# A spectral filter and a low-rank mixer on one core: which engine issues batch 1's spectrum stores, and in which slot its loads back stand

## The chip, the core and the metric

The kernel runs on one core of a Trainium2 chip. The core has five instruction streams that run side by side and meet only at semaphores: TensorE (PE), which multiplies matrices into PSUM banks; VectorE (DVE), ScalarE (ACT) and GpSimd (POOL), which compute elementwise; and SyncE (SP), which here does nothing but issue DMA transfers. ACT and POOL can issue DMA transfers too. Each stream is executed in order: an instruction that waits holds everything behind it on the same stream, and a DMA issue is such an instruction.

The metric is the device time of one execution in microseconds (us), as the median of several runs.

## What is computed

`x` has 8 batches of 3136 positions and 256 channels. The reference filters each channel in the frequency domain along the 3136 positions, and then applies a low-rank mixer along the positions and an MLP along the channels:

```python
X = np.fft.rfft(x, axis=1)
Y = X * (filt_r + 1j * filt_i)[None, :, :]
y = np.fft.irfft(Y, n=3136, axis=1)
u = y + (y.transpose(0, 2, 1) @ U @ V).transpose(0, 2, 1)      # rank 32
out = u + np.maximum(u @ w_ch1, 0.0) @ w_ch2                   # 256 -> 1024 -> 256
```

## The kernel before

**The transform.** 3136 is 64 x 49. A transform along the positions is done as a 64-point stage, a 49-point stage with the twiddle factors in its matrices, the filter, and the two stages back. For batches 1 to 7 the steps are these:

1. `f1_units`: PE multiplies a batch's `xt` tiles by the 64-point matrix (`pf`), ACT or DVE copies the result to `asb`, and a DMA stores it in the DRAM tensor `c1`. The stores of batch 1 are issued by SP, those of the later batches by POOL.
2. `load_a` (lines 466 to 470): SP loads a quarter of it back in another order, as one of three `a2` tiles (98 partitions x 8 frequencies x 256 channels), in two transfers, one of 96 partitions and one of 2. A quarter, number `gi` of 4, is 8 of the 32 frequency classes `NS`.
3. `stream` (lines 515 to 546): for each of 16 steps `m`, so 4 steps to a quarter, PE does the 49-point stage (`px`, line 488), DVE multiplies by the filter (`uv`), from batch 2 on POOL adds two halves (`y`), and PE does the 49-point stage back (`pi`, line 524). `pi` runs `LAG` = 2 steps behind `px`. ACT copies `pi` to one of two `esb` tiles (line 528), and behind the fourth copy of a quarter `esb` is stored in the DRAM tensor `c2`, again as one transfer of 96 partitions and one of 2 (line 531). This is the spectrum store.
4. `load_e` (lines 472 to 481): SP loads the quarter back in another order into the tiles `e2`, in three transfers (two at line 476, one at line 481). It can start only when both parts of the spectrum store have landed.
5. `h1_unit` (lines 552 to 589): when all four quarters of `e2` are there, PE projects them on the rank of the mixer (`ph`, line 566, 49 matmuls), ACT scales that (`h1`), PE folds it (`pn`), ACT copies it (`hz`), and DVE and four SP transfers spread it over further partitions of `e2` (lines 577 to 588).

Batch 0 does all this within the core's memory (`first_f1`, `first_mid`) before the main loop.

**The main loop** (lines 849 to 868) goes through the batches in groups of 4 row blocks. For each group, `make_u` forms `ut` with the last transform stage and the mixer (`u_part`, line 609), `mm1` does the first half of the MLP into 8 tiles `h` (line 683, ReLU on ACT at line 691), and `mm2` the second half of the group before (line 709 or 754). The result goes through DVE to `och` and by DMA to `out`.

**The order.** Instructions are recorded as the program writes them, and each engine executes its own in this order; no scheduler moves them. What belongs to the transform of later batches is woven into the main loop by hand, through numbered slots: `put(slot, ...)` files a piece of work and `run(slot)` records it. A group has 8 slots, a batch 48 (`SB`), and slots 0 to 47 lie under batch 0's MLP. For the work around the change the slots are these: the last copy of batch 1's quarters and with it the spectrum store at slots 14, 19, 25 and 30 (`steps`, line 809, and `put(t, mid)`); batch 2's `load_a` at slots 19, 29, 39 and 48 (line 832); `h1_unit` of batch 1 from slot 39 on (line 817); and batch 1's `load_e` where lines 821 to 828 put it, with `b` = 0 in that place (it counts the batches of the stream from 0):

```python
if k >= LAG and m % GP == GP - 1:
    t += 6 if b > 1 else 4 if b else 2
    late = SB * b + 13
    if b and t < late:
        ...
    else:
        put(t, one(load_e, b + 1, m // GP))
```

So `load_e` of batch 1 stands in slots 16, 21, 27 and 32, two behind its store.

SP's stream in this stretch is, in order: `load_a` of batch 1's first three quarters; store 0; `load_a` of batch 1's fourth quarter; e 0; store 1; `load_a` of batch 2's quarter 0; e 1; store 2; e 2; `load_a` of batch 2's quarter 1; store 3; e 3; `load_a` of batch 2's quarter 2. A store waits for ACT's copies, an e for the landing of its store, and `load_a` of batch 2's quarter 0 for the landing of batch 2's `c1` stores. Every transfer that SP or ACT issues signals its landing on one of eight completion semaphores, which the program gives out in turn, and it is not issued before the transfer that had this semaphore last has landed.

Of the kernel before, what the change touches and what calls it, by code (L numbers as in the profile page):

```python
# [16 lines left out]
DM = 256  # L17
# [72 lines left out]
def kernel(  # L90
# [11 lines left out]
    nc = tc.nc  # L102
# [11 lines left out]
    c2 = [nc.dram_tensor(f"c2_{b}", (64, RD), F16, kind="Internal") for b in range(nb)]  # L114
# [7 lines left out]
    def bank(tag, name):  # L122
        return ps.tile([128, 512], F32, tag=tag, bufs=BUFS[tag], name=name)
# [14 lines left out]
    def natural(ap):  # L138

        return ap.rearrange("p (r i h a) -> p r h i a", i=4, h=2, a=32)  # L140

    def split(ap):

        return ap.rearrange("p (r h i a) -> p r h i a", i=4, h=2, a=32)
# [318 lines left out]
    def spec(t, gi, p, n):  # L463
        return bass.AP(tensor=t, offset=gi * KG * 2 * RD + p * DM, ap=[[DM, n], [2 * RD, KG], [1, DM]])
# [18 lines left out]
    def forward(m, a2, xtags):  # L483
        ml = m % (KG // 2)
        px = bank(xtags[m % len(xtags)], "px")
        for sl in range(2):
            s = 2 * m + sl
            nc.tensor.matmul(px[:, sl * DM:(sl + 1) * DM], t2[:, s * 128:(s + 1) * 128],  # L488
                             a2[:, (2 * ml + sl) * DM:(2 * ml + sl + 1) * DM],
                             start=True, stop=True, skip_group_check=True)  # L490
        return px
# [23 lines left out]
    def stream():  # L515
        pend = []

        def i1(b, m, y, esb):
            pi = bank("f", "pi")
            nf = 2 if b == 1 else 1  # L520
            for sl in range(2):
                for fi in range(nf):
                    g, o = (4 * m + 2 * sl + fi) * 98, fi * 512 + sl * DM
                    nc.tensor.matmul(pi[0:98, sl * DM:(sl + 1) * DM], g12[:, g:g + 98],  # L524
                                     y[:, o:o + DM], start=(fi == 0), stop=(fi == nf - 1),
                                     skip_group_check=True)
            gi, ml = divmod(m, KG // 2)
            nc.scalar.copy(split(esb[:, ml * 512:(ml + 1) * 512]), natural(pi[0:98, :]))  # L528
            if ml == KG // 2 - 1:
                for p, n in ((0, 96), (96, 2)):  # L530
                    nc.sync.dma_start(spec(c2[b], gi, p, n),
                                      esb[p:p + n].rearrange("p (k d) -> p k d", d=DM))

        for b in range(1, nb):
            for m in range(NS // 2):
                gi, ml = divmod(m, KG // 2)
                if ml == 0:
                    esb = sb.tile([98, KG * DM], F16, tag="esb", bufs=2, name="esb")
                y = (both_products if b == 1 else product)(m, forward(m, st[b]["a"][gi], ("x",)))
                if len(pend) == LAG:  # L540
                    i1(*pend.pop(0))
                pend.append((b, m, y, esb))
                yield
        for p in pend:
            i1(*p)
            yield

    def one(load, *a):
        load(*a)
        yield  # L550
# [227 lines left out]
    def put(slot, gen):  # L778
        sched.setdefault(int(slot + 0.5), []).append(gen)
# [6 lines left out]
    NP = NS // 2  # L786
# [31 lines left out]
    for k, t in enumerate(steps):  # L818
        put(t, mid)
        b, m = divmod(k - LAG, NP)  # L820
        if k >= LAG and m % GP == GP - 1:
            t += 6 if b > 1 else 4 if b else 2
            late = SB * b + 13
            if b and t < late:
                put(max(t, SB * b - 1), one(load_e, b + 1, m // GP, (0,)))
                put(late, one(load_e, b + 1, m // GP, (1,)))
            else:
                put(t, one(load_e, b + 1, m // GP))
    for b in range(1, nb):
        for gi in range(NS // KG):  # L830
            t = steps[NP * (b - 1) + GP * gi]
# [67 lines left out]
```

## Time and profile before

| what | value |
|---|---|
| median of 3 runs | 538.48 us (536.94 to 539.28) |
| the profiled execution | 540.42 us |
| its span, first to last instruction | 537.5 us |
| granted TensorE clock, mean over the span | 0.983 |
| DMA moved, share of the 16 engines busy | 94.58 MB; 38.4% by POOL's queue, 37.8% by SP's |

How to read the profile. The first lines of its page give the span and each engine's busy time. PEld is the weight load of TensorE, which overlaps its matmuls. The chain of waits follows the work that ended last back through whatever released each step; a piece "DMA c<-esb" is the time from the issue of that transfer to its landing. The timeline lists an engine's instructions in order of time: start, duration, engine, line, operation, output and input by the program's tile names without their numbers (so `c` is `c1` or `c2`, `e` is `e2`, `a` is `a2`), shapes and count; a bracket at the end gives the idle time in front of it and what ended it. SPq stands for the stream of SP, whose instructions are DMA issues: their duration is that of the issue, not of the transfer. The view by windows gives for each stretch of time its length, the busy time and number of instructions of PE, PEld, DVE, ACT and POOL in this order, the granted TensorE clock (1.00 is full speed), the mean busy share of the 16 DMA engines and the GB/s that they moved. All times in these views count from the first instruction.

### The profile page before, as it was taken

The numbers are of one execution on the slowest core, as the hardware profiler recorded it, in microseconds if no ns is written. First come the engines' busy times: TensorE is split into PE (matmuls) and PEld (weight loads), VectorE is DVE, ScalarE is ACT, GpSimd is POOL, SyncE is SP. The second block draws the span as 40 slices with busy tenths as digits, with TensorE's granted clock in tenths as the row PEclk, the third lists the DMA queues.
The fourth block names the chain that finished last, engine by engine and source line by source line (L and its number), as shares of the span: only waits on it lengthen the run. The fifth ranks groups of instructions, "written<-read, shape, count | busy, mean of one in ns | idle before, by whom it ended". The sixth has DMA issues, their size and how long they took to land.

```text
span 537.5 us, 11370 instructions
## 1 busy us (share of the span) xinstructions
PE 501.6 (93%) x4022; PEld 305.5 (57%) x4022; DVE 396.5 (74%) x567; ACT 380.0 (71%) x777; POOL 287.9 (54%) x406
## 2 busy tenths in 40 slices
PE   3865899988999999999999999999999999999995
PEld 3754467755776776555555555555554555454444
DVE  6885377773787766888898878887999887335663
ACT  2666866764877867888888778888787777765541
POOL 7776553434466444676668567684756565313000
PEclk9889999997999999999999999999999999999999
DMA  8999999856988758896979798896876584643324
GB/s 132 189 198 209 181 203 222 215 158 178 203 210 208 196 121 236 189 243 142 249 196 235 185 187 215 207 229 161 201 184 153 126 193 115 141 105 80 75 67 104
DMA packets 118426, 94.58 MB, mean 176 GB/s; under 512 B 52961, under 2 KB 100770, under 8 KB 118370
## 3 DMA queue, kind: packets, MB, share of 16 engines
q0 software_dynamic: 21936, 42.52, 38.4%
q1 hardware_dynamic: 96434, 51.35, 37.8%
q8 instruction: 31, 0.51, 0.4%
q14 instruction: 25, 0.20, 0.1%
HBM read 56.85 MB, written 48.17 MB: 195 GB/s over the span
## 4 chain that ended last, share of the span: by engine, by line
PE 74%; DMA 10%; DVE 6%; ACT 3%; POOL 3%; issue 2%; SPq 1%; DVEq 0%; POOLq 0%; ACTq 0%
PE phh L683 26%; PE po L754 20%; PE po L709 7%; PE px L488 5%; PE pi L524 4%; PE pu L609 4%; DMA c<-esb 3%; DVE uv L509 3%; PE pf L449 3%; DMA xt<-in_x_dram 2%; PE ph L566 2%; DMA a<-c 2%; DMA g<-gd 1%; DMA c<-asb 1%; DVE uv L507 1%
## 5 line engine op out<-in xcount | busy, mean ns | idle before, releaser
L691 ACT ACTIVATE h<-phh 128x512 f16<-128x512 f32 (+1 forms) x391 | 205.6, 578 | 71.9 <-PE phh L683 68.9
L683 PE MATMUL phh<-ut,w 128*128 128x512 f16 x768 | 198.3, 380 | 0.9 <-ACT ut L676 0.5
L512 POOL TENSOR_TENSOR y<-uv 128x512 f16<-128x512 f16 x96 | 111.2, 1159 | 118.7 <-DVE uv L509 84.9
L754 PE MATMUL po<-h,w 128*128 128x512 f16 x560 | 143.8, 379 | 0.0
L509 DVE TENSOR_TENSOR uv<-px,ft 64x512 f16<-64x512 f32 x192 | 132.1, 688 | 2.6
L683 PEld LDWEIGHTS <-w 128*128 128x128 f16 x832 | 78.6, 98 | 78.1 <-issue 3.5
L507 DVE TENSOR_TENSOR uv<-px,ft 128x512 f16<-128x512 f32 x96 | 65.3, 680 | 48.7 <-PE px L488 42.9
L772 POOL DMA_DIRECT2D out_dram<-och x120 | 70.5, 594 | 40.7 <-DVE och L764 36.9
L528 ACT CAST esb<-pi 98x512 f16<-98x512 f32 x112 | 65.9, 589 | 36.3 <-PE pi L524 33.6
L754 PEld LDWEIGHTS <-w 128*128 128x128 f16 x560 | 51.6, 98 | 53.2 <-issue 1.1
L763 DVE TENSOR_TENSOR tt<-po,ut 128x512 f32<-128x512 f32 x70 | 48.4, 692 | 32.5 <-PE po L754 30.8
L709 PE MATMUL po<-w,h 128*128 128x256 f16 x448 | 58.7, 274 | 0.0
L488 PE MATMUL px<-a,t 98*128 98x256 f16 x256 | 50.0, 277 | 7.7 <-DVE uv L509 3.6
L455 ACT CAST asb<-pf 128x512 f16<-128x512 f32 (+1 forms) x83 | 48.1, 580 | 9.2 <-PE pf L449 8.2
L764 DVE STREAM_TRANSPOSE och<-tt 128x512 f32<-128x512 f32 x70 | 49.8, 711 | 2.4
L709 PEld LDWEIGHTS <-h 128*128 128x128 f16 x448 | 42.9, 99 | 10.8 <-issue 1.4
L496 DVE TENSOR_TENSOR uv<-px,ft 128x1024 f16<-128x1024 f32 x32 | 38.4, 1222 | 12.2 <-PE px L488 11.8
L488 PEld LDWEIGHTS <-t 98*128 98x128 f16 x256 | 22.9, 100 | 35.0 <-DVE uv L509 11.8
L449 PE MATMUL pf<-xt,w 128*128 128x512 f16 (+1 forms) x91 | 34.8, 384 | 5.6 <-DMA xt<-in_x_dram 4.4
L673 ACT CAST ut<-pu 128x512 f16<-128x512 f32 x70 | 38.1, 609 | 0.0
L524 PE MATMUL pi<-y,g 128*98 128x256 f16 x192 | 36.9, 273 | 0.7 <-POOL y L512 0.7
L153 POOL DMA_DIRECT2D xt<-in_x_dram x50 | 30.3, 613 | 4.2 <-DMA xt<-in_x_dram 1.6
(92 smaller groups left out, 440.9 us busy)
## 6 DMA issues: line engine op xcount, KB each, us to landing
xt<-in_x_dram POOLq DMA_DIRECT2D x46, 256.0 KB, 6.5
a<-c SPq DMA_DIRECT2D x28, 384.0 KB
c<-esb SPq DMA_DIRECT2D x28, 384.0 KB
e<-c SPq DMA_DIRECT2D x56, 192.0 KB
out_dram<-och SPq DMA_DIRECT2D x160, 64.0 KB
c<-asb POOLq DMA_DIRECT2D x30, 256.0 KB, 4.8
out_dram<-och POOLq DMA_DIRECT2D x120, 64.0 KB, 3.3
out_dram<-och POOLq DMA_DIRECT2D x24, 256.0 KB, 4.5
```

The costliest lines, as they stand in the source:

```text
L449: nc.tensor.matmul(pf[:, 0:w], w64[:, :], xt[:, n0 * DM:n0 * DM + w], start=True, stop=True)
L488: nc.tensor.matmul(px[:, sl * DM:(sl + 1) * DM], t2[:, s * 128:(s + 1) * 128], a2[:, (2 * ml + sl) * DM:(2 * ml + sl + 1) * DM], start=Tru ...
L507: nc.vector.tensor_mul(uv[:, 0:512], px[:, :], ft[:, a:a + 512])
L509: nc.vector.tensor_mul(uv[p:p + 64, 512:1024], px[q:q + 64, :], ft[q:q + 64, b:b + 512])
L512: nc.gpsimd.tensor_add(y, uv[:, 0:512], uv[:, 512:1024])
L524: nc.tensor.matmul(pi[0:98, sl * DM:(sl + 1) * DM], g12[:, g:g + 98], y[:, o:o + DM], start=(fi == 0), stop=(fi == nf - 1), skip_group_che ...
L528: nc.scalar.copy(split(esb[:, ml * 512:(ml + 1) * 512]), natural(pi[0:98, :]))
L683: nc.tensor.matmul(pm[:, 0:w], w1[:, dh * 1024 + t * 128:dh * 1024 + (t + 1) * 128], ut[:, dh * w:(dh + 1) * w], start=(dh == 0), stop=(dh ...
L691: nc.scalar.activation(h[:, 0:w], pm[:, 0:w], RELU)
L709: nc.tensor.matmul(po[:, o:o + DM], hs[gx, t][:, rr * 128:(rr + 1) * 128], w2[:, t * DM:(t + 1) * DM], start=(t == 0), stop=False, skip_gr ...
L754: nc.tensor.matmul(po[:, :], w2[:, t * DM + dh * 128:t * DM + (dh + 1) * 128], hs[gx, t][:, :], start=(t == 0), stop=(t == 7))
L772: (nc.gpsimd if k and b < nb - 1 else nc.sync).dma_start(dst, och[32 * i:32 * i + 32, k * 512:(k + 1) * 512] .rearrange("p (r e) -> p r e" ...
```

## The change

The spectrum stores of batch 1 are issued by ACT, right behind the copy that fills the tile, instead of by SP; those of the later batches stay with SP. And batch 1's `load_e` stands six slots behind the store for the first three quarters and four for the last, instead of two for all: slots 20, 25, 31 and 34 instead of 16, 21, 27 and 32. Nothing is added or taken away, and PE, DVE and POOL keep their order.

```diff
@@ i1(), in stream()
             nc.scalar.copy(split(esb[:, ml * 512:(ml + 1) * 512]), natural(pi[0:98, :]))
             if ml == KG // 2 - 1:
                 for p, n in ((0, 96), (96, 2)):
-                    nc.sync.dma_start(spec(c2[b], gi, p, n),
-                                      esb[p:p + n].rearrange("p (k d) -> p k d", d=DM))
+                    (nc.scalar if b == 1 else nc.sync).dma_start(
+                        spec(c2[b], gi, p, n), esb[p:p + n].rearrange("p (k d) -> p k d", d=DM))
@@ the main part
         if k >= LAG and m % GP == GP - 1:
-            t += 6 if b > 1 else 4 if b else 2
+            t += 6 if b > 1 or not b and m < NP - 1 else 4
```

SP's stream in this stretch becomes: `load_a` of batch 1's four quarters; `load_a` of batch 2's quarter 0; e 0; e 1; `load_a` of batch 2's quarter 1; e 2; e 3; `load_a` of batch 2's quarter 2. In ACT's stream two DMA issues stand behind the fourth, eighth, twelfth and sixteenth copy of `esb`. The completion semaphores are dealt out in turn as before, now over both streams, which gives these waits beside those for the data: store 3 on ACT waits for the landing of `load_a` of batch 2's quarter 0 and of the first transfer of e 0; on SP the third transfer of e 0 waits for store 1, and `load_a` of batch 2's quarter 1 waits for store 2.

## The prediction

> **What bounds the kernel now.** I read the page first, then the chain of waits, then TensorE's timeline around the place where the chain leaves TensorE, and last the streams of SP and ACT in front of it.
>
> ```profile
> span 537.5 us, 11370 instructions
> ...
> PE 501.6 (93%) x4022; PEld 305.5 (57%) x4022; DVE 396.5 (74%) x567; ACT 380.0 (71%) x777; POOL 287.9 (54%) x406
> ...
> PE   3865899988999999999999999999999999999995
> ...
> PEclk9889999997999999999999999999999999999999
> ```
>
> The span is 537.5 us and the execution took 540.42, so 2.9 us lie around it. PE is busy for 93%; of its 40 slices (13.4 us each) those from the eleventh on stand at 9 up to the last. Two slices at 8 stand before them (107.5 to 134.4 us), and in the second of these the granted clock is 0.7, which it is nowhere else after the start. So TensorE sets the time, with one hole in the middle. The chain of waits says what made it:
>
> ```profile
> 99.20 10.69 DMA c<-esb
> ...
> 113.59 5.09 DMA c<-esb
> ...
> 119.35 3.60 DMA e<-c
> ...
> 122.99 2.29 PE ph L566 x37
> ```
>
> The chain goes through store 2 (99.20 and 10.69 more, so landed at 109.89), store 3 (issued 113.59, landed 118.68), a transfer of e 3 (landed 122.95) and into `ph`. PE's timeline shows what that costs:
>
> ```profile
> 101.15 0.60 PE L524 MATMUL pi<-uv,g 128*98 128x256 f16 x4
> ...
> 118.02 0.38 PE L488 MATMUL px<-a,t 98*128 98x256 f16 x2 [0.27 <-DMA a<-c]
> ...
> 122.06 0.51 PE L566 MATMUL ph<-e,ul 64*32 64x256 f16 x12 [2.23 <-DMA e<-c]
> 122.99 2.29 PE L566 MATMUL ph<-e,ul 64*32 64x256 f16 x37 [0.42 <-DMA e<-c]
> ```
>
> `ph` needs all four quarters of e. It began at 122.06 after 2.23 us of idle time and stopped once more for 0.42; shortly before, `px` waited 0.27 for `load_a` of batch 2. The row of 101.15 is used below. The view by windows gives the price behind the hole:
>
> ```profile
> 119.80:122.06 2.26, 0.03 (x2) 0.01 (x2) 1.48 (x3) 0.00 (x0) 1.29 (x2) 1.00 0.57 170
> 122.06:125.25 3.19, 2.77 (x50) 1.86 (x51) 0.00 (x0) 0.00 (x0) 1.94 (x4) 0.62 0.78 211
> 125.25:130.00 4.75, 4.75 (x22) 2.81 (x22) 2.10 (x4) 3.02 (x6) 0.00 (x0) 0.54 0.52 184
> ```
>
> Full speed until the gap, then 0.62 over 2.77 busy us and 0.54 over 4.75: lost are 2.77 x 0.38 + 4.75 x 0.46 = 1.05 + 2.19 = 3.24 us. With the 2.65 us of waiting, the hole costs 5.9 us.
>
> **Why e 3 was late.** SP's stream:
>
> ```profile
> 80.75 0.74 SPq L531 DMA_DIRECT2D c<-esb  x2
> ...
> 84.62 1.50 SPq L476 DMA_DIRECT2D e<-c  x2
> ...
> 88.89 0.95 SPq L531 DMA_DIRECT2D c<-esb  x2
> 92.93 0.94 SPq L469 DMA_DIRECT2D a<-c  x2
> 97.28 1.19 SPq L476 DMA_DIRECT2D e<-c  x2
> ...
> 99.20 1.56 SPq L531 DMA_DIRECT2D c<-esb  x2
> 109.90 1.19 SPq L476 DMA_DIRECT2D e<-c  x2
> ...
> 112.37 1.12 SPq L469 DMA_DIRECT2D a<-c  x2
> 113.59 1.75 SPq L531 DMA_DIRECT2D c<-esb  x2
> 118.70 1.73 SPq L476 DMA_DIRECT2D e<-c  x2
> 120.47 0.59 SPq L481 DMA_DIRECT2D e<-c  x1
> ```
>
> Between 99.20 and 109.90 SP issued nothing: it stood at e 2, waiting for store 2 to land. The waits of SP name it, the longest 9.1 us:
>
> ```profile
> SPq L476 <- DMA c<-esb: 19.7, 5, 9.1
> SPq L469 <- DMA c<-asb: 8.3, 3, 3.6
> ```
>
> Behind it in the stream stood e 2's third transfer, a `load_a` and store 3. Store 3 was issued at 113.59, but ACT had filled its tile long before:
>
> ```profile
> 80.12 0.61 ACT L528 CAST esb<-pi 98x512 f16<-98x512 f32 x1
> 81.79 0.59 ACT L528 CAST esb<-pi 98x512 f16<-98x512 f32 x1 [1.06 <-PE pi L524]
> ...
> 88.28 0.59 ACT L528 CAST esb<-pi 98x512 f16<-98x512 f32 x1 [0.77 <-PE pi L524]
> 89.14 0.60 ACT L691 ACTIVATE h<-phh 128x512 f16<-128x512 f32 x1 [0.28 <-PE phh L683]
> ...
> 92.12 0.59 ACT L528 CAST esb<-pi 98x512 f16<-98x512 f32 x1 [1.21 <-PE pi L524]
> ...
> 98.24 0.59 ACT L528 CAST esb<-pi 98x512 f16<-98x512 f32 x1 [0.67 <-PE pi L524]
> ...
> 99.97 0.59 ACT L528 CAST esb<-pi 98x512 f16<-98x512 f32 x1 [0.16 <-ACT h L691]
> ...
> 107.50 0.59 ACT L528 CAST esb<-pi 98x512 f16<-98x512 f32 x1
> 108.92 1.08 ACT L691 ACTIVATE h<-phh 128x512 f16<-128x512 f32 x2 [0.83 <-PE phh L683]
> ```
>
> The last copies of the four quarters end at 80.73, 88.87, 98.83 and 108.09 (start plus duration). So store 3 lay ready for 113.59 - 108.09 = 5.5 us, and e 3 was late by 2.65 us.
>
> **The change, part by part.**
>
> *Store 3 on ACT.* It goes out at about 108.1 instead of 113.6. Until it lands: the four stores before were followed by their e after 84.62 - 80.75 = 3.87, 8.39, 10.70 and 5.11 us, and the DMA engines were nearly idle just then:
>
> ```profile
> 108.00:112.00 4.00, 4.00 (x33) 2.76 (x31) 3.05 (x5) 2.62 (x6) 2.17 (x3) 1.00 0.25 59
> ```
>
> A share of 0.25 stands nearest to the 3.87 and 5.11 cases, so I take 5 and a landing at 113.1; the ends are 112.0 and 118.8.
>
> *Store 2 and what SP has behind it.* Store 2 goes out at 98.9 instead of 99.20. I leave it its 10.7 us: landed at 109.6. SP is by then through with e 0 and e 1, and `load_a` of batch 2's quarter 1, which waits for store 2 by its semaphore, goes out at 109.6, 2.8 us earlier than before (112.37). It lasts 1.2 us (112.37 to 113.59), e 2 lasts 2.5 (109.90 to 112.37), so e 3 can be issued from 113.3 on, with store 3 landed by then. From its issue to `ph`'s last wait it took 122.95 - 118.70 = 4.25 us: e 3 is there at 117.6. PE comes to `ph` at 119.8, so 2.2 us are to spare, the 2.23 and the 0.42 are gone, and with no hole the clock has no reason to fall. The 0.27 goes too, its transfer being issued 2.8 us earlier. Sum of the gain: 2.65 + 3.24 + 0.27 = 6.16 us. The other end is store 3 at 118.8: e 3 at 123.05 and nothing gained.
>
> *e 0 and e 1 later, `load_a` earlier.* e 0 moves from 84.62 to behind the `load_a` of 92.93, which waits for batch 2's own `c1` stores (longest 3.6 us), so to about 94. Its third transfer stands until store 1 lands (before 97.28), e 1 follows at about 98. Nobody reads them before `ph` at 119.8; that cover is 20 us, so the moves cost nothing by themselves. What they bring is traffic: e 0's three transfers now run beside store 2. That could lengthen the 10.7 us: e 0 moves 8 x 98 x 256 values of 2 bytes, 0.40 MB, which at the mean rate of the execution (94.58 MB in 537.5 us) are 2.3 us. If all of that fell on store 2, e 3 would be there at 119.9, a wait of 0.1 us; the other end is none of it. Batch 1's fourth `load_a` is no longer behind store 0 and can only come earlier. POOL's stream keeps its order.
>
> *The stores on ACT.* Eight issues move into ACT's stream, two behind each last copy, and behind them stand the ReLUs and copies that free PSUM banks for PE. Their length on SP:
>
> ```profile
> L469 SPq DMA_DIRECT2D a<-c x15: 314/534/1986, 61.6 to 134.9; - x15
> ...
> L531 SPq DMA_DIRECT2D c<-esb x10: 313/387/1399, 80.8 to 129.2; - x10
> ```
>
> No row shows one on ACT. The pairs on SP took 0.74 to 1.75 us, from the first issue to the end of the second. What ACT had free behind each: 1.06 us before 81.79; 0.28 before 89.14 and 1.21 more before 92.12; 0.16 before 99.97, and PE's next `pi` into the same single bank came at 101.15, 0.59 after that copy ended; 0.83 before 108.92. With pairs of 0.95 us PE loses 0 + 0 + 0.20 + 0.12 = 0.3 us, with 1.75 it loses 0.69 + 0.26 + 1.00 + 0.92 = 2.9. ACT has no other transfers queued, so the price lies near the short pairs; I take 0.6. The waits for semaphores on ACT are for transfers issued at 92.93 and about 94, some 14 us ahead of store 3: covered. If `load_a` were late by as much, ACT would stand, and with it PE.
>
> *Sum.* 6.16 - 0.6 = 5.5 us. Against the profiled execution: 540.42 - 5.5 = 534.9. That execution lies 1.94 above the median of the runs shown (538.48), so for the median: 533.0. Behind the hole PE's slices stand at 9 and its clock at 9 up to the tail: no later wait there is waiting to swallow the gain, and what the other engines do follows PE by data, so I expect it to reach the end.
>
> **The rivals.**
>
> *A. The hole stays.* The transfers, not SP's stream, are what is late: store 3 takes 10.7 us beside the added traffic, e 3 lands at 123.05 as before, and only ACT's 0.6 is new: 539.1. For it: POOL's transfers share the engines, and 8.39 and 10.70 did happen. Against it: the 0.25 share at 108 to 112 and the 5.5 us for which store 3 lay ready. The Trainium skill speaks for this rival: its page "DMA: Bandwidth & Descriptors", section "Issuing engines are not separate DMA queues", says that starting transfers from several engines saves only the sequencer's time for the issue, usually little beside the transfer. By that rule nothing but the pairs of 0.74 to 1.75 us would be won on SP, and the hole would stay. The trace bears that out for the transfers but not for the stream: what SP loses is 9.1 us of waiting, not of issuing.
>
> *B. A shorter hole.* e 3 lands about 1.2 us after PE arrives, since store 2 takes 14 us. The clock then falls or it doesn't: 6.16 - 1.2 - 0.6 = 4.4 gives 534.1; without the 3.24 it is 1.1 and 537.4.
>
> *C. The clock falls all the same.* If the low clock isn't the hole's doing, 2.65 + 0.27 - 0.6 = 2.3 us are gained: 536.2. Against it stands the row of 119.80 with 1.00 beside the two that follow. The Trainium skill's page "TensorE: Matmul & The Clock Gate", section "Why this matters for your kernels", advises no idle gap over about 3 us, after which the clock is halved; by it a gap of 2.23 us should have left the clock alone, and this rival would be the forecast. The trace shows the fall 0.8 us behind the end of that shorter gap (0.62 over 3.19 us is 0.77 at full and the rest at half speed), and the measurement decides.
>
> *D. ACT is held by its issues: slower.* If each of the eight takes the longest that SP's loads of the same size show, 1.99 us, a pair costs 3.98 less what ACT had free (1.06, 1.49, 0.75, 0.83): 11.8 us lost, 6.16 gained, 544.1. It decides from pairs of 3.25 us on ((6.16 + 2.7 + 4.13) / 4). For it: ACT is 71% busy and in order. Against it: the median issue of a store is 387 ns.
>
> **How the numbers follow.** Under 0.5%, 2.7 us, this kernel's runs can't be told from no change, so faster is below 535.8 and slower above 541.2. The forecast has 0.68; its own range is 6.16 - 0.3 to 6.16 - 2.9 of gain, 532.6 to 535.2. A has 0.09 (same), B 0.11 (half faster, half same), C 0.03 (same), D 0.09 (slower). Faster: 0.68 + 0.06 = 0.74; same: 0.09 + 0.05 + 0.03 = 0.17; slower 0.09. The range goes down to 531.0 (532.6 less the 1.5 us by which the fastest run lay below the median) and up to 537.5, B's worse half and C within it; A and D are left out.
>
> **What would show it.** Right: PE goes from the `px` rows into `ph` without an idle bracket; the slice at 121 to 134 us has its full clock; SP's wait for `c<-esb` is short at e 3; store 3 is issued from ACT within a microsecond of the sixteenth copy. The issues on ACT last 0.3 to 0.9 us, and the copy behind store 2 begins up to a microsecond late. Wrong: an idle bracket before line 566 that names `e<-c` (A, B); a clock of 0.5 without one (C); idle brackets at `pi` or `phh` that name ACT between 80 and 112 us, and issues on ACT of over 1.6 us (D); or the gain is there at 130 us and gone by the end, at a wait that no row of before shows.

## The result, and the profile after

| | before | after |
|---|---|---|
| median | 538.47 us (22 runs, 533.91 to 542.51) | 533.75 us (22 runs, 529.26 to 538.98) |
| the profiled execution | 540.42 us, span 537.5 | 529.26 us, span 527.2 |
| mean granted clock | 0.983 | 0.997 |

The ratio after to before is 0.9905 [0.9882, 0.9927]: 3.9 to 6.4 us faster, and 4.7 by the medians. The profiled execution of after is the fastest of its 22, so its span overstates the gain, and the stretch in which the change acts has to be cut out first. For a later set of runs (after_again, slots_again and slots_keep below) the ratio counts only those of before's runs that lie near its fastest, and as that one lay unusually low (531.03) it leaves out half of them, so there the medians over all runs are given too.

The page of after begins thus (the rows of slices have 40 equal pieces of the span, 13.2 us each here):

```profile
span 527.2 us, 11361 instructions
...
PE 498.6 (95%) x4022; PEld 304.1 (58%) x4022; DVE 396.0 (75%) x567; ACT 378.8 (72%) x777; POOL 286.7 (54%) x406
...
PE   3877899999999999999999999999999999999995
...
PEclk9998999999999999999999999999999999999999
```

PE stands at 9 from the sixth slice to the last but one, and the 7 in the clock row at 121 to 134 us of before is a 9. PE's timeline goes into `ph` with no idle bracket, nor is there one at `px` (start, duration, work, and in a bracket the idle time in front):

```profile
64.67 1.03 PE L683 MATMUL phh<-ut,w 128*128 128x512 f16 x4 [0.31 <-ACT h L691]
...
115.27 0.38 PE L488 MATMUL px<-a,t 98*128 98x256 f16 x2
...
117.00 1.79 PE L566 MATMUL ph<-e,ul 64*32 64x256 f16 x49
118.73 1.04 PE L683 MATMUL phh<-ut,w 128*128 128x512 f16 x4
...
125.24 0.64 PE L609 MATMUL pu<-low,e 96*128 96x64 f16 x16
```

The same view of before has the first and the last of these so:

```profile
66.92 1.02 PE L683 MATMUL phh<-ut,w 128*128 128x512 f16 x4 [0.31 <-ACT h L691]
...
133.87 0.66 PE L609 MATMUL pu<-low,e 96*128 96x64 f16 x16
```

These two rows are landmarks: the last short wait for ACT ahead of the change, and the first `pu` matmuls on batch 1's result. Between them lie 133.87 - 66.92 = 66.95 us before and 125.24 - 64.67 = 60.57 after. So the change saved 6.4 us in its own stretch. The 2.25 us by which after reached the first landmark earlier, and the 1.7 by which the rest was shorter (403.6 against 402.0), are not its doing. I call the time between the landmarks the stretch and use it below for every kernel. Windows around `ph` in after (length; busy us of PE, PEld, DVE, ACT, POOL; granted clock, DMA share, GB/s):

```profile
117.07:118.79 1.72, 1.69 (x50) 1.14 (x51) 1.46 (x3) 0.01 (x1) 0.77 (x1) 1.00 0.46 86
118.79:125.00 6.21, 6.21 (x47) 4.16 (x46) 4.05 (x6) 5.15 (x11) 4.98 (x8) 1.00 0.73 193
```

Full speed throughout; before had 0.62 and 0.54 here. The chain of waits, which in before came through stores 2 and 3 and e 3 into `ph`, stays on PE:

```profile
116.96 0.11 PE po L713 x2
117.07 0.44 PE ph L566 x12
117.51 0.03 issue
117.53 1.26 PE ph L566 x36
118.79 0.97 PE phh L683 x4
```

No transfer is left in it. ACT's timeline shows the stores (ACTq is the stream of ACT, here with its DMA issues):

```profile
77.79 0.61 ACT L528 CAST esb<-pi 98x512 f16<-98x512 f32 x1
78.42 1.02 ACTq L531 DMA_DIRECT2D c<-esb  x2
...
95.91 0.58 ACT L528 CAST esb<-pi 98x512 f16<-98x512 f32 x1 [0.68 <-PE pi L524]
96.52 0.82 ACTq L531 DMA_DIRECT2D c<-esb  x2
...
105.17 0.58 ACT L528 CAST esb<-pi 98x512 f16<-98x512 f32 x1
105.79 0.83 ACTq L531 DMA_DIRECT2D c<-esb  x2
```

Each pair goes out some 0.03 us behind its last copy (105.17 + 0.58 = 105.75, issued at 105.79), where store 3 used to lie for 5.5. SP's stream, and its longest wait for a spectrum store that batch 2's `load_a` names:

```profile
96.73 0.50 SPq L481 DMA_DIRECT2D e<-c  x1
97.29 2.75 SPq L476 DMA_DIRECT2D e<-c  x2
100.08 0.61 SPq L481 DMA_DIRECT2D e<-c  x1
107.90 0.76 SPq L469 DMA_DIRECT2D a<-c  x2
108.71 1.19 SPq L476 DMA_DIRECT2D e<-c  x2
...
110.58 1.59 SPq L476 DMA_DIRECT2D e<-c  x2
112.21 0.59 SPq L481 DMA_DIRECT2D e<-c  x1
```

```profile
SPq L469 <- DMA c<-esb: 7.1, 1, 7.1
```

SP still stands for 7.1 us until store 2 lands, now at a `load_a` by the shared semaphore (107.90). But store 3 is no longer behind it, and e 3 goes out at 110.58, right behind e 2's last issue (109.94 + 0.59 = 110.53). So store 3 had landed by then, at most 4.8 us after its issue, where the prediction took 5.

### The profile page after: what moved, and what is told of

It is laid out like the page before. It is cut to its first block, busy times and chain, and to the rows that moved or that the text cites. A ratio compares the mean times of both kernels' runs of the same rounds, so it can differ in the third digit from the quotient of the medians.

```text
span 527.2 us, 11361 instructions
## 1 busy us (share of the span) xinstructions
PE 498.6 (95%) x4022; PEld 304.1 (58%) x4022; DVE 396.0 (75%) x567; ACT 378.8 (72%) x777; POOL 286.7 (54%) x406
## 4 chain that ended last, share of the span: by engine, by line
PE 80%; DVE 5%; DMA 4%; ACT 4%; POOL 3%; issue 2%; DVEq 0%; SPq 0%; POOLq 0%; ACTq 0%
PE phh L683 28%; PE po L754 21%; PE po L709 8%; PE px L488 5%; PE pi L524 5%; PE pu L609 4%; DVE uv L509 3%; PE pf L449 3%; DMA xt<-in_x_dram 2%; PE ph L566 2%; DVE uv L507 1%; DMA c<-asb 1%; PE po L713 1%; ACT a L378 1%; DMA ft<-in_filt_r_dram 1%
```

## The experiments

The theory is the prediction's: store 3 was ready and stood in SP's stream behind e 2, which waited for store 2; e 3 and `ph` were late by that, and the idle time brought the clock down (call this last part K). Rivals are A (the transfers themselves were late; B, a shorter hole, is its milder form, and after has no hole left), C (the clock falls whatever PE does) and D (ACT pays for its issues). A further question is which half of the edit does it: the engine or the slots.

In the table, the ratio, with its 95% interval, is against before on the same chip; it is not the quotient of the two medians, which are over all runs. The stretch is that of the one profiled execution, between the same two landmarks.

| kernel | median, us | before there | ratio | stretch, us |
|---|---|---|---|---|
| before | | | | 66.95 |
| after | 533.75 | 538.47 | 0.9905 [0.9882, 0.9927] | 60.57 |
| slots_only | 533.09 | 538.72 | 0.9892 [0.9854, 0.9930] | 60.36 |
| act_only | 534.78 | 538.72 | 0.9896 [0.9853, 0.9939] | 66.00 |
| store3_act | 535.69 | 538.72 | 0.9930 [0.9905, 0.9954] | 61.08 |
| store3_sp | 537.92 | 538.72 | 0.9961 [0.9924, 0.9997] | 67.78 |
| e2_behind | 533.96 | 538.06 | 0.9899 [0.9859, 0.9939] | 60.36 |
| before_busy | 535.99 | 538.06 | 0.9953 [0.9921, 0.9984] | 63.58 |
| quarter_parts | 537.29 | 538.06 | 0.9976 [0.9944, 1.0009] | 65.78 |
| a22_first | 535.98 | 538.06 | 0.9954 [0.9927, 0.9981] | 64.71 |
| after_again | 533.68 | 538.96 | 0.9929 [0.9893, 0.9965] | 60.72 |
| slots_again | 533.95 | 538.96 | 0.9918 [0.9887, 0.9948] | 60.36 |
| slots_keep | 533.61 | 538.96 | 0.9963 [0.9924, 1.0002] | 63.95 |

The stretches of store3_sp and quarter_parts hold, at their very start, a wait of 0.92 and 1.19 us of batch 1's first `px` for its `load_a`, which has nothing to do with the stores; without it they are 66.86 and 64.59. That of slots_keep has 2.14 of the same kind.

**Which half: act_only and slots_only.** `act_only` is after with the slots of before, `slots_only` is before with the slots of after:

```diff
 act_only, against after
-            t += 6 if b > 1 or not b and m < NP - 1 else 4
+            t += 6 if b > 1 else 4 if b else 2
 slots_only, against after
-                    (nc.scalar if b == 1 else nc.sync).dma_start(
+                    nc.sync.dma_start(
```

> Batch 1's stores on ACT as in the changed kernel, its loads back in the slots of before (16, 21, 27, 32). Theory H (SP's stream held store 3 behind e 2, and that alone made the hole at line 566): store 3 goes out within 0.5 us of the sixteenth copy, e 3's last transfer lands before PE reaches ph, no idle bracket before line 566, 532 to 535 us, 4 to 6 under before. Theory T (the gain comes from e 0 and e 1 being moved, so from the order of the loads): the hole stays at 2 us or more, 537 to 539.

> Batch 1's stores on SP as before, its loads back in the slots of the changed kernel (20, 25, 31, 34). Store 3 (slot 30) then stands ahead of e 2 (slot 31) in SP's stream. Theory H: nothing holds store 3 any more, so the hole is gone as in the changed kernel, 532 to 535 us. Rival S (the gain needs ACT's own DMA queue, in which a store does not stand behind SP's loads): store 2 or 3 lands later than in the changed kernel, the hole is 1 us or more, 536 to 539.

`slots_only` has the whole gain with every store on SP: a stretch of 60.36 us and no bracket at `px` or `ph`. Its SP stream, and its row of `ph`:

```profile
101.20 3.89 SPq L469 DMA_DIRECT2D a<-c  x2
109.53 0.74 SPq L531 DMA_DIRECT2D c<-esb  x2
110.63 1.19 SPq L476 DMA_DIRECT2D e<-c  x2
```

```profile
120.75 1.59 PE L566 MATMUL ph<-e,ul 64*32 64x256 f16 x49
```

Store 3 went out at 109.53, within 0.03 us of its copy's end, because nothing in front of it on SP waited for store 2 any more. So another engine isn't needed; what counts is that no wait stands ahead of store 3 in its stream. `act_only` lost the hole at `ph`, but its profiled execution, the longest of the six at 540.97 us, had one of the same kind shortly before it, at `px`:

```profile
122.43 0.38 PE L488 MATMUL px<-a,t 98*128 98x256 f16 x2 [2.15 <-DMA a<-c]
```

On SP, batch 2's `load_a` still stood behind e 2, which waited for store 2, and was issued at 114.98. That execution gained next to nothing (a stretch of 66.00 against 66.95), while the median of the six is 534.78, within H's range. Since the six runs go from 529.71 to 540.97, I read no more from this profile than the place of the wait; whether the faster runs have it too is not known.

**One store alone: store3_act and store3_sp.** Both are before with some of batch 1's stores on ACT: only store 3, or all but store 3.

```diff
 store3_act
-                    nc.sync.dma_start(
+                    (nc.scalar if b == 1 and gi == 3 else nc.sync).dma_start(
 store3_sp
+                    (nc.scalar if b == 1 and gi < 3 else nc.sync).dma_start(
```

> Before, with only the last of batch 1's four stores (two DMA issues) on ACT; all slots and the other stores as before. Theory H: this single store is what was held, so the gain is whole: no idle bracket over 0.5 us before line 566, 532 to 535 us. Theory T: e 0, e 1 and e 2 stand as before, so the hole stays, 537 to 539.

> Slots as before, stores 0 to 2 on ACT, only store 3 on SP. Theory H: store 3 is again issued behind e 2 and a load, 4 to 6 us after the sixteenth copy, and the hole at line 566 is back at 1.5 to 3 us with the clock at half behind it: 537 to 539 us. Rival S: stores 0 to 2 have their own queue and land earlier, so e 2 is earlier and the hole shrinks to under 1 us: 534 to 536.

PE's timeline of `store3_act` has one idle bracket in the whole stretch beyond those at its start, and the clock stays whole:

```profile
119.48 0.38 PE L488 MATMUL px<-a,t 98*128 98x256 f16 x2 [0.57 <-DMA a<-c]
```

That of `store3_sp` is before's again, with the half clock behind it in the windows:

```profile
121.34 0.51 PE L566 MATMUL ph<-e,ul 64*32 64x256 f16 x12 [2.20 <-DMA e<-c]
122.34 2.08 PE L566 MATMUL ph<-e,ul 64*32 64x256 f16 x37 [0.49 <-DMA e<-c]
```

```profile
122.60:129.40 6.80, 6.80 (x57) 4.15 (x46) 2.35 (x4) 3.01 (x6) 0.83 (x3) 0.50 0.68 225
```

Store 3 was issued there at 113.60, 5.8 us behind its copy. So one store of the four decides about the hole at `ph`. The 0.57 that `store3_act` has left at `px` is the `load_a` that only the slots bring forward; it accounts for its stretch (60.36 + 0.57 = 60.9, measured 61.08). The median, 535.69, is above H's 532 to 535, so in time the gain is not shown to be whole: it is 3.0 us by the medians, where `slots_only` has 5.6, and the 0.7 by which the two stretches differ doesn't explain that. `store3_sp` came out as H has it, 537.92. Against A: with store 3 early, no transfer kept `ph` waiting.

**One load alone: e2_behind.** Before, with only e 2 four slots later (31 instead of 27), which puts it behind store 3; all stores stay on SP.

```diff
-            t += 6 if b > 1 else 4 if b else 2
+            t += 6 if b > 1 or not b and m == 11 else 4 if b else 2
```

> Before, with e 2 alone moved, from slot 27 to slot 31, behind batch 2's second load_a and store 3; all stores on SP. Theory H: the one load that made SP wait in front of store 3 no longer does, store 3 goes out within 1.5 us of the sixteenth copy, no hole at line 566 and none at px: 532 to 535 us. Rival S (ACT's queue is needed): hole of 1 us or more, 536 to 539.

SP's stream shows the new order, store 3 at 113.36 ahead of e 2:

```profile
104.34 1.06 SPq L531 DMA_DIRECT2D c<-esb  x2
105.45 6.40 SPq L469 DMA_DIRECT2D a<-c  x2
113.36 0.75 SPq L531 DMA_DIRECT2D c<-esb  x2
115.16 1.19 SPq L476 DMA_DIRECT2D e<-c  x2
...
117.38 1.43 SPq L476 DMA_DIRECT2D e<-c  x2
```

No bracket at `px` or `ph` and a stretch of 60.36: moving a single load does it all. The two issues of `load_a` took 6.40 us here (5.83 of it one issue; why is open), which did no harm, since they ended 1.5 us before store 3 was ready (its copy ended at 113.33).

**Does the gap bring the clock down: before_busy.** Before, with 40 matmuls of 128 columns in front of batch 1's `ph`, into an unused half of its bank. They are extra work whose results nobody reads; they only keep PE busy while e 3 is under way (`ph` stands three lines lower).

```diff
+        for k in range(40 if b == 1 else 0):
+            nc.tensor.matmul(ph[:, 256 + k % 2 * 128:384 + k % 2 * 128], w64[:, :], idn[:, :],
+                             start=True, stop=True, skip_group_check=True)
```

> Before, with 40 matmuls of 128 columns put in front of batch 1's ph, into the unused half of its PSUM bank, so that PE works while it waits for e 3. They add work of about 2.3 us, all inside the wait. Theory K (the low clock is the hole's doing, 3.2 of its 5.9 us): the granted clock stays at 1.00 behind ph and the time falls by 2.5 to 3.5 us to 535 to 536, though e 3 comes no sooner. Rival C (the clock falls there anyway): the 0.5 stretch behind ph stays, 538 to 539.

PE's timeline, and the window from the start of `ph` on:

```profile
124.32 2.40 PE L559 MATMUL ph<-idn,w 128*128 128x128 f16 x40
126.72 0.51 PE L569 MATMUL ph<-e,ul 64*32 64x256 f16 x12
127.83 1.25 PE L569 MATMUL ph<-e,ul 64*32 64x256 f16 x37 [0.60 <-DMA e<-c]
```

```profile
126.72:136.00 9.28, 8.68 (x112) 6.13 (x113) 4.75 (x7) 5.82 (x12) 4.67 (x7) 1.00 0.79 236
```

PE is as late as before (2.40 of useless work and 0.60 of waiting), but at full speed from there on, and the kernel is faster than before although it does more. The stretch shrank by 66.95 - 63.58 = 3.4 us and the median by 2.1, against K's 3.24 less 0.35 (3.00 us late instead of 2.65). So C has fallen: at the same place, with e 3 as late, the clock stays whole when PE is kept busy.

**What the issues cost on ACT: quarter_parts.** After, with each store of batch 1 in four transfers, so that blocks of four issues stand on ACT.

```diff
-                for p, n in ((0, 96), (96, 2)):
+                for p, n in ((0, 32), (32, 32), (64, 32), (96, 2)) if b == 1 else ((0, 96), (96, 2)):
```

> The changed kernel with each of batch 1's stores cut into four transfers (32, 32, 32 and 2 partitions), so 16 issues on ACT instead of 8. By the pairs of the changed kernel (0.82 to 1.02 us) four issues last some 1.8 us. Theory P (an issue on ACT costs PE what exceeds ACT's free time behind it, 1.06, 1.49, 0.75 and 0.83): 0.7 + 0.3 + 1.05 + 1.0 = 3 us slower than the changed kernel, 536 to 537.5, with idle brackets of PE at pi or phh that name ACT. Rival F (ACT makes it up later and PE doesn't notice): 533 to 535.

The blocks took 2.02, 2.28, 2.96 and 1.75 us. Only the one behind store 2 reached PE; ACT's timeline and then PE's:

```profile
99.42 2.96 ACTq L531 DMA_DIRECT2D c<-esb  x4
102.43 1.08 ACT L691 ACTIVATE h<-phh 128x512 f16<-128x512 f32 x2 [3.04 <-PE px L488]
```

```profile
104.04 0.60 PE L524 MATMUL pi<-uv,g 128*98 128x256 f16 x4 [2.16 <-ACT esb L528]
```

By the prediction's cover the four blocks should have cost 2.02 - 1.06, 2.28 - 1.49, 2.96 - 0.75 and 1.75 - 0.83, that is 1.0, 0.8, 2.2 and 0.9. The third is nearly met (2.16), and the others cost nothing that PE shows; why ACT's lateness is caught up there was not tested. Behind the 2.16 the clock stood at 0.50 for 3.40 us, another 1.7. The median is 3.5 us above after's, the two together 3.9 (the stretch: 64.59 - 60.57 = 4.0). So D's mechanism exists, and begins at that one place, but pairs of 0.82 to 1.02 us hardly reach it.

**How thin the margin is: a22_first, after_again, slots_again.** `a22_first` is after with batch 2's third `load_a` ahead of e 3 instead of behind it. The other two are after and `slots_only` once more, side by side: after's e 3 lands just after PE comes to `ph`, that of `slots_only` 2.3 us ahead of it by the trace.

```diff
 a22_first, against after
-            put(max(0, t - (14 if b > 3 else 9 + b // 3)), one(load_a, b, gi))
+            put(33 if (b, gi) == (2, 2) else max(0, t - (14 if b > 3 else 9 + b // 3)), one(load_a, b, gi))
```

> The changed kernel with batch 2's third load_a put ahead of e 3 in SP's stream (slot 33 instead of 39), which puts two issues, some 1.1 us, and 0.4 MB of traffic in front of e 3. In the changed kernel the last transfer of e 3 landed at 117.7 us, 0.6 after PE's first ph matmul, so nothing is to spare. Theory H: e 3 lands 1 to 2.5 us later and a hole of 0.5 to 2 us is back at line 566. If the clock stays at 1.00 behind so short a hole: 534.5 to 536; if it halves: 537 to 538.5. Rival T (the transfers overlap and e 3 is no later): 533 to 534.

> The changed kernel once more, on the same chip as the next two. Theory H: as first measured, 4 to 6.5 us under before, 532 to 535. If its e 3 has nothing to spare, as its profile showed (117.7 us against ph at 117.1), some executions have a rest of the hole and it lies 0.5 to 2 us above slots_again; if that margin is enough, both are the same within 0.3%.

> The loads moved and the stores left on SP, beside the changed kernel. In its first profile e 3 landed 2.3 us ahead of ph, and batch 2's second load_a was issued at 101.2 instead of 107.9 us, since it didn't share a completion semaphore with store 2. Theory H with the thin margin: 0.5 to 2 us under after_again. Without: the same within 0.3%.

In `a22_first` the hole is back in PE's timeline, and the window behind it has the half clock:

```profile
99.95 0.60 PE L524 MATMUL pi<-uv,g 128*98 128x256 f16 x4 [0.26 <-ACT esb L528]
120.30 2.01 PE L566 MATMUL ph<-e,ul 64*32 64x256 f16 x49 [2.28 <-DMA a<-c]
```

```profile
121.50:124.90 3.40, 3.40 (x26) 1.70 (x16) 0.02 (x1) 1.69 (x4) 0.69 (x2) 0.50 0.91 247
```

(`ph` reads no `a`; the releaser is inferred, and by the trace e 3 landed from 120.21 on.) One load ahead of e 3 costs 2.28 us of waiting and 1.7 of clock, and 0.26 went to ACT behind store 2: 4.2 in all, where the stretch grew by 64.71 - 60.57 = 4.1. The median, 535.98, is only 2.2 above after's and lies in the range that was expected for a whole clock (534.5 to 536), not in that for a halved one (537 to 538.5): the traced execution lost more than the median run did. In that trace, at least, there was no room for another transfer. But as it stands the thin margin costs nothing: `after_again` and `slots_again` have medians of 533.68 and 533.95.

**A better version? slots_keep.** `slots_only`, with 36 idle matmuls (extra work, read by nobody) in a wait of PE at the end of batch 0's transform, in the hope that a whole clock there would save what the hole at `ph` had cost.

```diff
+        keep = bank("f", "keep")
+        for k in range(36):
+            nc.tensor.matmul(keep[:, k % 4 * 128:k % 4 * 128 + 128], w64[:, :], idn[:, :],
+                             start=True, stop=True, skip_group_check=True)
```

> slots_again with 36 matmuls of 128 columns on PE in front of the transposes of batch 0 at about 46 us, where PE waits 1.8 to 4.4 us for ACT in every profile and the clock halves in most. Theory K (a hole is paid twice, in waiting and in the clock behind it): the half-speed stretch at 49 to 56 us goes, 1 to 2.5 us under slots_again, 530 to 532.5. Rival: PE isn't the bound there and nothing is gained, or the 36 matmuls cost up to 1 us.

PE's timeline:

```profile
46.94 2.17 PE L426 MATMUL keep<-idn,w 128*128 128x128 f16 x36 [0.42 <-ACT et L398]
...
68.54 0.59 PE L492 MATMUL px<-a,t 98*128 98x256 f16 x2 [2.14 <-DMA a<-c]
```

The wait is filled and the clock is whole from there to 68.4 us, where `slots_again` had half clock from 49.6 to 56.5. But PE comes earlier to batch 1's first `px`, where it waits 2.14 us for its `load_a`, and from there the clock is at 0.50 for 3.4 us. The median, 533.61, is that of `slots_again`, and the expected 530 to 532.5 was missed: in the traces, the first landmark came 3.5 us earlier than in `slots_again` (65.37 and 68.90), and the stretch was 3.6 longer. No kernel here is faster than after beyond what the runs can tell; `e2_behind` and `slots_only` equal it with less edited.

## Why the prediction was right

**The cause.** The named place, wait and order were all borne out. `store3_act` and `store3_sp` single out store 3, and `e2_behind` singles out the load that held it. For rival A, the Trainium skill's rule ("DMA: Bandwidth & Descriptors", "Issuing engines are not separate DMA queues"), by which another issuing engine saves only the time of the issue, does not cover what counted here: a wait at the head of an in-order stream is not issue time, and both another engine for one store (`store3_act`) and another order on the same engine (`slots_only`) took store 3 out from behind it.

**The sum.** Of 6.16 us of gain, the 2.65 of waiting, the 3.24 of clock and the 0.27 at `px` are all gone in after's rows, and the stretch shrank by 6.38. The medians moved by 4.7, where 5.5 was predicted; in the last set they moved by 5.3 (538.96 to 533.68), but the ratio there gives 3.8 (1.9 to 5.8). The hole of the one profiled execution of before is thus deeper than what the runs lost on average. That the time came out so near owes something to luck: the 0.6 taken off for ACT was hardly paid, and the runs gained less than the trace has. Whether the hole varies from execution to execution wasn't measured: only one execution of each is traced.

**ACT's 0.6 was too much.** The issues were as short as assumed (pairs of 0.82 to 1.02, predicted near 0.95), but no bracket of PE in after names ACT between 68 and 139 us. The 0.20 put down behind store 2 is the one part that was met, as 0.26 in `a22_first`, with after's issues on ACT. The estimate of 0.3 to 2.9 treated every microsecond beyond ACT's free time as lost on PE; `quarter_parts` shows that this holds behind store 2 alone. After's stretch is 0.21 us above that of `slots_only`, which bounds ACT's price and the thin margin together.

**The margin of 2.2 us was not there.** Put on before's time scale by adding the 2.25 of the first landmark, `load_a` went out at 110.2 (predicted 109.6, store 2 taking 11.4 us instead of 10.7), and e 3 at 112.8 (predicted 113.3), so SP's part came out. But e 3 then took longer than the 4.25 us carried over from before. The weight loads of `ph` in after have the last trace of that wait:

```profile
117.53 0.98 PEld L566 LDWEIGHTS <-ul 64*32 64x32 f16 x37 [0.31 <-DMA e<-c]
```

`ph` began at 117.00, and behind its first 12 matmuls the weight loads waited 0.31 us for e, unseen on PE. So e 3 was there only at 117.5, 6.9 us after 110.58; in `after_again` the same row has a wait of 0.43. The window of its flight shows what it flew through:

```profile
110.00:116.00 6.00, 5.88 (x45) 3.70 (x43) 3.54 (x6) 4.22 (x9) 2.30 (x2) 1.00 1.03 286
```

The DMA engines were full (share 1.03; by this count it can pass 1): two `load_a` and two e were issued between 107.90 and 113.5, where before e 3 had flown through a quieter stretch (0.39 from 118.70 to 123.14). The duration of a transfer had been taken from a place that the change itself filled up. The stores on ACT have a part in that: in after `load_a` shares its completion semaphore with store 2 and goes out at 107.90, just ahead of e 2 and e 3, while in `slots_only` it doesn't and went out at 101.20. That the missing margin cost nothing was luck: one load more, in `a22_first`, and the hole was back.

**The clock.** Rival C drew on the Trainium skill's advice ("TensorE: Matmul & The Clock Gate", "Why this matters for your kernels") of no idle gap over about 3 us. Here gaps of 2.14 to 2.28 us were each followed by a half clock, in before, `store3_sp`, `act_only`, `quarter_parts`, `a22_first` and `slots_keep`, and filling before's gap (`before_busy`) removed it. The measurement decides.

## What to carry to other kernels

A DMA that waits on an in-order issuing stream also holds the ready ones behind it; put loads that must wait for a landing behind the stores that are ready, and first ask whether moving one instruction does it (`e2_behind`) before moving work to another engine. A wait of 2 us on a busy TensorE has to be priced with the clock behind it, which here was another 1.7 to 3.4 us (1.7 behind 2.28, 3.24 behind 2.65, 3.4 behind the 2.20 and 0.49 of `store3_sp`). And a transfer's duration may only be carried over to its new place if the DMA engines are as free there.

## What the runs showed of the hardware

- Behind these gaps the half clock came in two lengths: about 3.4 us in `quarter_parts`, `a22_first` and `slots_keep`, about 6.8 in before, `store3_sp` and `act_only`, always at 0.50. The gaps were alike (2.14 to 2.28 us, in before and `store3_sp` with a second one of 0.42 and 0.49 behind). What decides between one and two such pieces was not settled. Gaps of 0.57 us (`store3_act`), 0.60 (`before_busy`) and 1.19 (`quarter_parts`) brought none. The length of the gap alone doesn't decide: ahead of the stretch, `a22_first` has gaps of 1.84 and 1.13 us (up to 48.92 and 51.58) with a whole clock behind them, and after has gaps of 1.75 and 1.13 (up to 46.58 and 49.24) with half clock from 49.2 to 52.6.
- Executions of one kernel differ by some 9 us (before: 533.91 to 542.51). In the profiles much of this lies ahead of the change, where half clock cost PE about 4.5 us in before's and 1.7 in after's: the first landmark came at 64.67 to 72.24 us over the kernels with an unchanged start, while the stretch came out at 60.36 three times (`slots_only`, `slots_again`, `e2_behind`). To compare single profiles, two landmarks around the change tell far more than the spans do.
